# Another order of the fixed places in SBUF: parts and sums of activations three 64-byte lines under the weights

## The chip, the cores and the metric

The kernel runs on one NeuronCore of a Trainium2 chip. The metric is the time of one execution on the device in microseconds (us), lower is better; 0.2% of it is 1.3 us.

## The reference, cut to what matters

Causal attention over a window of 96 keys plus 8 global keys, with a slope per head, for 4 batches of 768 tokens and 8 heads of 64; its output, 3072 tokens of 512 features, goes through two matrix products with an ELU between them.

```python
scores = q @ k.T / 8 + bias          # 4 x 8 heads, 768 x 768, kept: 96 back or the first 8
a = softmax(where(keep, scores, -1e9))
x = (a @ v) laid out as 3072 x 512
h = x @ w_in                         # 512 -> 2048
g = where(h > 0, h, exp(min(h, 0)) - 1)
out = g @ w_out                      # 2048 -> 512
```

## The kernel before, in words

**Precision.** Every float32 operand of the two large products is split into a high part (`HI`, fp32r) and a rest (`LO` or "l"), and three of the four products of parts are added in PSUM. So x lives as `xh` and `xl`, each weight row block as one tile of 2 x 512 values, and the activations as pairs too.

**Tiling.** The 3072 tokens are 12 groups of 256. d_ff = 2048 is 16 blocks of 128 (`fc`). "Up" for one block (`mm1`) is 12 matmuls of 256 columns: the weights `w1` are the stationary operand (128x128), x is the moving one. "Down" makes the activations stationary and streams the second weights. Groups 0 to 3 use `moe` (up on L856, down on L885 with 512 moving columns, activations in `gh`, `gl`). Groups 4 to 11 use `seven` (up on L713, down on L769): two blocks make a pair, whose 2x2 products of quarters are formed with seven products, from activations in `rh`, `rl` (parts) and their sums in `sh`, `sl`, and from weights or mixes of weights (`mix`). A pair is 24 up matmuls and then 21 down matmuls of 256 columns; 8 groups have 64 pairs. Attention visits (values on L611, scores on L475) come in between, in the middle of an up or a down stretch.

**Order.** `Plan.order` is a list scheduler: it knows costs, due times and, for every class of tile, a list of named places (`SLOTS`). A tile takes the place that comes free first, ties by name. It never sees an address. The instructions are then issued in that order on every engine, under a manual schedule.

**Addresses.** Two pools lie behind each other in SBUF: `w` with the 32 weight tiles of 4096 bytes per partition, and `m`. `places_in_sbuf` allocates in `m` one tile per entry of `PLACES`, in the order of that list, so the list fixes the address of each name. Counted in bytes per partition, modulo 512: the weights and `pa0` to `pa5` (mixes of weights among them) start at the same remainder. `qk0` has 2496 bytes, which is 39 lines of 64 bytes, one line less than a multiple of 512. So each place from `xh0a` to `ph2` starts one line under the weights. The names that matter:

- `xh0*`, `xh1*`, `xl0*`, `xl1*`: x of groups 0, 1 and of groups 4 to 11 in turn
- `x0`, `ph2`, `rk0`, `va0`: x of group 3 (and sums before they are cast, scratch of attention)
- `xh2*`, `xl2*`: x of group 2; from group 4 on `sh` and `sl`
- `gh0` to `gh2`, `gl0` to `gl2`: `gh` and `gl`; from group 4 on `rh` and `rl`

Of the kernel before, what the change touches and what calls it, by code (L numbers as in the profile page):

```python
# [246 lines left out]
class Kernel:  # L247
# [686 lines left out]
    def build(self):  # L934
# [63 lines left out]
        for _, f in sorted(todo, key=lambda x: x[0]):  # L998
# [5 lines left out]
    LATE, FIRST_LOADS = 12, 22  # L1004
    RESUMED = 4
    PLACES = (("pa0", 2048), ("pa1", 2048), ("pa2", 2048), ("pa3", 2048), ("pa4", 2048), ("pa5", 2048), ("qk0", 2496), ("xh0a", 2048), ("xh0b", 2048),
# [5 lines left out]
    PREPARE, SE = (168000.0, 9000.0, 6000.0), 4  # L1012
    OF = ({1: (0, 0), 2: (0, 1), 6: (1, 0), 5: (1, 1), 3: (2, 0), 7: (2, 1), 4: (3, 0)}, {1: (0, 0), 4: (0, 1), 6: (1, 0), 7: (2, 0), 2: (3, 0), 5: (4, 0), 3: (5, 0)})
    ON_PE = []
# [355 lines left out]
```

## Time and profile before

| | us |
|---|---|
| runs, median (lowest to highest of 3) | 634.79 (634.67 to 634.83) |
| profiled execution, its own time | 634.52 |
| its span, first to last instruction | 632.7 |
| PE busy | 621.9 |

The span is what the trace holds; 1.8 us of the profiled execution lie around it. In the tables PE is TensorE's matmul row and PEld its loads of stationary operands, which run beside the matmuls. "The chain" is the chain of work that ended last, followed back from the last instruction; in it a stretch of matmuls is told by the starts, so its length divided by its count is the time from one matmul to the next.

### The profile page before, as it was taken

What the parts mean: (1) busy time and instruction counts of PE and PEld (TensorE: products, weight loads), DVE (VectorE), ACT (ScalarE), POOL (GpSimd) and SP (SyncE); (2) the same over time, 40 slices, a digit from 0 to 9 for tenths busy, and PEclk for the clock granted to TensorE, in tenths of its full rate; (3) what the DMA queues carried; (4) which work ended last, traced back from release to release, by engine and by line L of the source; (5) the groups of instructions that cost most, each with busy time, mean ns of one, the idle gap of its engine ahead of it and who ended that gap; (6) DMA issues with size and microseconds to landing.
All of it is one profiled execution on the core that took longest, in us unless ns stands there. A gap on an engine that the chain in (4) does not pass through costs nothing.

```text
span 632.7 us, 19150 instructions
## 1 busy us (share of the span) xinstructions
PE 621.9 (98%) x7046; PEld 576.7 (91%) x7046; DVE 487.8 (77%) x1630; ACT 428.3 (68%) x1246; POOL 207.7 (33%) x491
## 2 busy tenths in 40 slices
PE   8999999999999999999999999999999999999995
PEld 5778888898898889999999999999999999999995
DVE  6899888878786877777877877877877877875755
ACT  5999778888656755667667667667667666655552
POOL 3645465656464784112112112112112112110000
PEclk9999999999999999999999999999999999999999
DMA  8979835322354899998898898998997997994542
GB/s 306 383 274 408 318 129 137 114 68 88 89 199 155 268 301 271 304 273 266 280 271 252 266 272 276 280 272 259 274 276 249 279 282 250 261 247 153 183 151 87
DMA packets 131171, 149.82 MB, mean 237 GB/s; under 512 B 63616, under 2 KB 82816, under 8 KB 131072
## 3 DMA queue, kind: packets, MB, share of 16 engines
q1 hardware_dynamic: 130784, 148.41, 74.9%
q8 instruction: 57, 0.93, 0.6%
q14 instruction: 42, 0.34, 0.2%
q10 hardware_dynamic: 288, 0.13, 0.1%
HBM read 117.57 MB, written 30.93 MB: 235 GB/s over the span
## 4 chain that ended last, share of the span: by engine, by line
PE 92%; DVE 3%; ACT 2%; issue 1%; DMA 1%; POOL 0%; ACTq 0%; DVEq 0%; POOLq 0%
PE h L713 28%; PE o L769 25%; PE h L856 13%; PE o L885 13%; PE s L611 5%; PE s L475 4%; PE pv L508 2%; PE t L528 1%; PE t L530 1%; DMA n_raw<-in_n_dram 1%; PE none L1141 1%; ACT pt L304 0%; ACT pr L465 0%; DVE g L397 0%; DVE hl L673 0%
## 5 line engine op out<-in xcount | busy, mean ns | idle before, releaser
L581 POOL TENSOR_SCALAR pr<-pr,st 128x168 f32<-128x168 f32 x144 | 74.1, 515 | 254.0 <-DVE st L483 197.5
L713 PE MATMUL h<-xh,w 128*128 128x256 f32 x1024 | 138.8, 278 | 0.0
L713 PEld LDWEIGHTS h<-xh,w 128*128 128x128 f32 x1024 | 127.7, 188 | 0.3
L723 DVE SCALAR_TENSOR_TENSOR gg<-e,h 128x256 f32<-128x256 f32 x128 | 53.6, 418 | 83.6 <-ACT e L722 83.5
L465 ACT ACTIVATE pr<-pr,nmax 128x168 f32<-128x168 f32 x192 | 82.8, 432 | 25.0 <-DVE nmax L463 24.7
L856 PEld LDWEIGHTS h<-xh,w 128*128 128x128 f32 x512 | 76.0, 188 | 9.8 <-DVE gl L312 0.6
L721 ACT ACTIVATE e<-h 128x256 f32<-128x256 f32 x128 | 49.0, 383 | 52.3 <-PE h L713 52.3
L885 PE MATMUL o<-w,gh 128*128 128x512 f32 x256 | 80.4, 399 | 0.4 <-ACT o L304 0.4
L856 PE MATMUL h<-xh,w 128*128 128x256 f32 x512 | 80.2, 282 | 0.2 <-DVE gl L312 0.2
L713 PE MATMUL h<-xl,w 128*128 128x256 f32 x512 | 79.8, 278 | 0.0
L713 PEld LDWEIGHTS h<-xl,w 128*128 128x128 f32 x512 | 68.3, 188 | 0.5 <-issue 0.2
L312 POOL TENSOR_TENSOR w<-g,w 128x256 fp32r<-128x256 f32 x64 | 50.2, 807 | 41.2 <-ACT w L304 20.5
L304 ACT CAST sh<-sum 128x512 fp32r<-128x512 f32 x64 | 39.9, 623 | 34.2 <-DVE sum L737 34.2
L463 DVE CUSTOM_DVE_ANT_0 pr<-s,far 128x168 f32<-128x168 f32 x192 | 53.5, 321 | 2.3 <-PE s L475 0.8
L722 ACT ACTIVATE e<-e 128x256 f32<-128x256 f32 x128 | 53.3, 416 | 2.8
L304 ACT CAST rh<-gg 128x384 fp32r<-128x384 f32 x64 | 33.0, 515 | 27.7 <-DVE gg L723 27.6
L586 DVE STREAM_TRANSPOSE tr<-pr 128x192 f32<-128x192 f32 x144 | 51.2, 366 | 0.5 <-POOL pr L581 0.3
L769 PE MATMUL o<-mix,sh 128*128 128x256 f32 x256 | 51.1, 281 | 0.0
L769 PE MATMUL o<-w,sh 128*128 128x256 f32 x256 | 50.6, 287 | 0.0
L312 DVE TENSOR_TENSOR sl<-sum,sh 128x512 fp32r<-128x512 f32 x64 | 43.7, 682 | 7.1 <-ACT sh L304 7.1
L885 PEld LDWEIGHTS o<-w,gh 128*128 128x128 f32 x256 | 42.9, 189 | 6.6 <-ACT o L304 0.8
L885 PE MATMUL o<-w,gl 128*128 128x512 f32 x128 | 45.0, 396 | 0.0
(141 smaller groups left out, 1390.7 us busy)
## 6 DMA issues: line engine op xcount, KB each, us to landing
mix<-mixed SPq DMA_DIRECT2D x192, 256.0 KB, 3.8
qk<-in_qkv_dram SPq DMA_DIRECT2D x48, 312.0 KB, 4.0
v<-in_qkv_dram SPq DMA_DIRECT2D x36, 384.0 KB, 4.8
dd<-tr SPq DMA_DIRECT2D x36, 384.0 KB, 4.1
pt<-dd SPq DMA_DIRECT2D x72, 192.0 KB, 4.0
bits<-in_w_in_dram SPq DMA_DIRECT2D x16, 512.0 KB, 7.6
bits<-in_w_out_dram SPq DMA_DIRECT2D x16, 512.0 KB, 9.4
mixed<-mix SPq DMA_DIRECT2D x32, 256.0 KB, 3.7
```

The costliest lines, as they stand in the source:

```text
L304: self.nc.scalar.copy(out, x)
L312: self.on(e).tensor_tensor(out, x, y, ALU.subtract)
L463: first = p.add((("DVE", 85 + 1.042 * LW, False),), lambda e: nc.vector.tensor_tensor_reduce(x(), s.t[:, i, :LW], tab, -(2.0 ** -(h + 1)), ...
L465: p.add(act(LW, extra=200), lambda e: nc.scalar.activation(x(), x(), AF.Exp, bias=nm, scale=-1.0, accum_out=st.t[:, n, 0:1]), [pr], [pr, s ...
L581: nc.gpsimd.tensor_scalar(pr.t[:, :LW], pr.t[:, :LW], st.t[:, n, 3:4], 1.0, ALU.mult, ALU.mult)
L586: nc.vector.transpose(tr.t[:, :, i, j], pr.t.rearrange("p (b r) -> p b r", r=32))
L713: nc.tensor.matmul(h.t, w1.t[:, s, cc * P:(cc + 1) * P], self.chunk(x, cc), start=n == 0 and s == HI and cc == 0, stop=n == 1 and cc == se ...
L722: p.add(act(W), lambda e: nc.scalar.activation(ex.t, ex.t, AF.Exp, scale=-1.0), [ex], [ex], d - 8000)
L723: p.add(dve(W), lambda e: nc.vector.scalar_tensor_tensor(gs(), ex.t, -1.0, h.t, ALU.add, ALU.max), [h, ex], [g], d - 8000)
L769: nc.tensor.matmul(acc[bank].t[:, half], a, b.t[:, LO if t == 1 else HI, x], start=j == 0 and t == 0 and n in first, stop=j == self.NFC // ...
L856: nc.tensor.matmul(h.t, w1.t[:, s, cc * P:(cc + 1) * P], self.chunk(x, cc), start=n == 0 and cc == 0, stop=n == 2 and cc == self.NCC - 1)
L885: nc.tensor.matmul(o.t[:, :at.stop - at.start], g.t[:, i * P:(i + 1) * P], w2.t[:, s, at], start=fc == f0 and n == 0 and s == HI and not r ...
```

## The change

Only the order of `PLACES` changes. The tiles of x of groups 0 and 1 and the five places `rk0`, `va0`, `x0`, `ph2`, `rqv0` come first, and `xh2*`, `xl2*`, `gh*`, `gl*` follow behind `rqv0`. Sizes, names, `SLOTS`, due times and the program are as before.

```diff
-    PLACES = (... ("qk0", 2496), ("xh0a", 2048), ("xh0b", 2048),
-             ("xh1a", 2048), ("xh1b", 2048), ("xh2a", 2048), ("xh2b", 2048), ("xl0a", 2048), ("xl0b", 2048), ("xl1a", 2048), ("xl1b", 2048),
-             ("xl2a", 2048), ("xl2b", 2048), ("gh0", 1536), ("gh1", 1536), ("gh2", 1024), ("gl0", 1536), ("gl1", 1536), ("gl2", 1024), ("rk0", 2048),
-             ("va0", 2048), ("x0", 2048), ("ph2", 2496), ("rqv0", 2496), ("tf0", 1024), ...
+    PLACES = (... ("qk0", 2496), ("xh0a", 2048), ("xh0b", 2048),
+             ("xh1a", 2048), ("xh1b", 2048), ("xl0a", 2048), ("xl0b", 2048), ("xl1a", 2048), ("xl1b", 2048), ("rk0", 2048), ("va0", 2048),
+             ("x0", 2048), ("ph2", 2496), ("rqv0", 2496), ("xh2a", 2048), ("xh2b", 2048), ("xl2a", 2048), ("xl2b", 2048), ("gh0", 1536),
+             ("gh1", 1536), ("gh2", 1024), ("gl0", 1536), ("gl1", 1536), ("gl2", 1024), ("tf0", 1024), ...
```

In front of the moved tiles there are now three tiles of 2496 bytes (`qk0`, `ph2`, `rqv0`) in place of one: 117 lines, three less than a multiple of eight. So `xh2*`, `xl2*`, `gh*` and `gl*` start three lines under the weights. `xl0*`, `xl1*` move by 4096 bytes and `rk0`, `va0`, `x0`, `ph2`, `rqv0` by 16384, both multiples of 512, and keep their remainder. Everything from `tf0` on stays where it was.

## Rows read from the trace of the kernel before

**Rows 1.** The page: span, busy time of PE, its clock by slices, the chain by engine.
```profile
span 632.7 us, 19150 instructions
...
PE 621.9 (98%) x7046; PEld 576.7 (91%) x7046; DVE 487.8 (77%) x1630; ACT 428.3 (68%) x1246; POOL 207.7 (33%) x491
...
PEclk9999999999999999999999999999999999999999
...
PE 92%; DVE 3%; ACT 2%; issue 1%; DMA 1%; POOL 0%; ACTq 0%; DVEq 0%; POOLq 0%
```

**Rows 2.** Busy time of each engine in two stretches: us, instructions, clock, DMA share, GB/s.
```profile
257.00:520.00 263.00, 263.00 (x3334) 255.26 (x3331) 203.24 (x737) 172.89 (x510) 51.52 (x176) 1.00 0.91 271
...
576.00:625.00 49.00, 48.97 (x422) 48.55 (x421) 31.23 (x92) 25.87 (x60) 0.00 (x0) 1.00 0.47 152
```

**Rows 3.** Groups of PE by line and shape: count, busy us, mean ns, idle before.
```profile
L713 PE MATMUL h<-xh,w 128*128 128x256 f32 x1024 | 138.8, 278 | 0.0
L885 PE MATMUL o<-w,gh 128*128 128x512 f32 x256 | 80.4, 399 | 0.4 <-ACT o L304 0.4
L856 PE MATMUL h<-xh,w 128*128 128x256 f32 x512 | 80.2, 282 | 0.2 <-DVE gl L312 0.2
...
L885 PE MATMUL o<-w,gl 128*128 128x512 f32 x128 | 45.0, 396 | 0.0
L856 PE MATMUL h<-xl,w 128*128 128x256 f32 x256 | 40.4, 280 | 0.0
...
L611 PE MATMUL s<-pt,v 64*64 64x64 f32 x1728 | 33.4, 222 | 0.0
```

**Rows 4.** The chain from 259 to 300 us: start, us, line and count.
```profile
264.22 0.94 PE h L713 x8
...
266.60 2.04 PE h L713 x16
268.63 2.38 PE o L769 x21
271.02 2.83 PE h L713 x24
273.85 2.47 PE o L769 x21
276.32 2.73 PE h L713 x24
279.05 1.70 PE o L769 x15
...
282.19 0.91 PE o L769 x6
283.09 2.73 PE h L713 x24
```

**Rows 5.** The chain from 575 to 634 us, after the last attention visit.
```profile
581.58 2.83 PE h L713 x24
584.41 2.47 PE o L769 x21
586.88 2.73 PE h L713 x24
...
608.04 2.73 PE h L713 x24
610.78 2.38 PE o L769 x21
613.16 2.83 PE h L713 x24
```

**Rows 6.** Groups of PE in the up stretch from 289.87 to 292.60 us.
```profile
L713 PE MATMUL h<-xh,w 128*128 128x256 f32 x16 | 2.1, 277 | 0.0
L713 PE MATMUL h<-xl,w 128*128 128x256 f32 x8 | 1.2, 276 | 0.0
```

**Rows 7.** Groups of PE in the next up stretch, from 294.98 to 297.81 us.
```profile
L713 PE MATMUL h<-xh,w 128*128 128x256 f32 x16 | 2.2, 281 | 0.0
L713 PE MATMUL h<-xl,w 128*128 128x256 f32 x8 | 1.3, 281 | 0.0
```

6 rows, old and new, of the table PLACES are left out of this document.

## The prediction

> **What bounds the kernel.** I began with the page. PE is busy for 621.9 of 632.7 us, the chain that ended last is 92% PE, and the granted clock is 9 in every slice, so TensorE keeps its upper level of 2.4 GHz [rows 1]. The stretches say the same: between 257 and 520 us PE never pauses, and near the end neither [rows 2]. The groups by line show no wait worth a term in front of the large matmuls (at most 0.4 us in all) [rows 3]. So nothing that another engine does is worth time here; what counts is how fast one matmul follows another. For that I read the chain as a list of stretches, and there the reader should see something odd: the same 24 up matmuls take 2.73 us in one pair and 2.83 in another, the same 21 down matmuls 2.38 or 2.47 [rows 4, 5]. Per matmul that is 113 to 114 ns against 118. I call these the quick and the slow pace. In a slow stretch the matmul itself is longer, 281 ns against 276 or 277, with no idle time before it [rows 6, 7]: the operand stream is held up.
>
> Three things about the two paces matter. **They last**: a stretch keeps its pace, and an up stretch hands it to the next down stretch (2.83 then 2.47) [rows 4, 5]. **They swap at the step from down to up**: a quick down (2.38) is followed by a slow up (2.83), a slow down (2.47) by a quick up (2.73), and after the last attention visit the pairs simply alternate [rows 5]. **A down that resumes after an attention visit is slow**, 0.91 us for 6 (152 ns each, the restart included), and a quick up follows; an up resumed after a visit ends 16 in 2.04 us and its down is quick [rows 4]. In the chain from 257 us to the end I count 59 up stretches of 24: 17 slow (the first at 271.02, the last at 613.16); 33 whole down stretches: 16 slow; and 28 visits that cut a stretch, one of them an up (of the 1728/48 = 36 visits [rows 3], the rest are earlier).
>
> **The change part by part.** *The program* is not touched: the planner sees names, no addresses, so all instructions, waits and DMA issues stay in their order on every queue. Nothing is added or removed, and no DMA reads or writes a moved tile. Cost 0 by construction. *ACT, DVE and POOL*, which write and read the moved tiles, see addresses that differ by a multiple of 64 bytes. I take 0; the cover is that PE waits for them 0.0 to 0.4 us per group [rows 3], and if a cast got slower by a few ns it would still be hidden. *TensorE's operands* are the only term. In lines of 64 bytes, modulo eight and counted from the weights: an up matmul has stationary 0 and moving -1, before and after (only group 2 gets moving -3). A down matmul has moving 0 and stationary -1 before, -3 after. So relative to the moving operand the stationary one goes from +1 (up) and -1 (down) to +1 and -3. The trace has only the first two, and both have a quick and a slow pace. No row shows what -3 does, so I bound it.
>
> Late part, from 257 us (64 pairs). A slow up costs 2.83 - 2.73 = 0.10 us, a slow down 2.47 - 2.38 = 0.09 [rows 4]. Below: all quick gives back 17 x 0.10 + 16 x 0.09 = 3.1 us. A visit inside a down costs 1.70 + 0.91 - 2.38 = 0.23, one inside an up 0.94 + 2.04 - 2.73 = 0.25 [rows 4], although the up is quick again soon; so hardly more than 0.03 of each is pace, 28 x 0.03 = 0.8. Together -3.9 us. Above: all slow adds (64 - 17) x 0.10 = 4.7 for the ups, 17 x 0.09 = 1.5 for the whole quick downs and, for the 28 cut ones, 15 x 0.0043 = 0.06 each, 1.8. Together +8.0 us.
>
> Early part (groups 0 to 3). The up matmuls of L856 average 282 and 280 ns [rows 3], at the slow 281 [rows 7], so there is little left to lose and 768 x 4.2 ns (0.10 us / 24) = 3.2 us to gain. The 384 down matmuls of L885 have no quick row to compare with; at the same 4.2 ns each they may give or take 1.6. Bounds -4.8 and +1.6 us. I take -0.6: runs of 4 to 8 matmuls switch often, as now, so I stay near zero.
>
> A pace quicker than 113 ns is in no row of 64 x 45 = 2880 late matmuls; I can't exclude it and leave it to the low end of the range.
>
> **What I take for the late part.** The step from down to up loads the same first weights (0) against the same moving operand (0), before and after. So I expect a quick down still to throw the next up into the slow pace. What is open is the step from up to down, where the first load reads line -3 over a stream of line -1, and whether -3 holds a slow pace. Three outcomes are near each other: pairs alternate as now (0); all ups quick and all downs slow, 64 x 0.09 = 5.8 against the present 3.9, +1.9; all ups slow and downs quick, 64 x 0.10 = 6.4, +2.5. Their mean is +1.5, with the early -0.6 it is +0.9 us. The sum is made against the profiled execution, 634.52 (span 632.7 and 1.8 around it); the median of the runs is 0.27 above it. 634.8 + 0.9 = **635.7 us**. This forecast's own range is 633.2 (alternating, early part -1.6) to 637.7 (late +2.5, early +0.4).
>
> **The rivals.**
>
> *All quick, faster.* If -3 leaves no place for the slow pace in a down, or the step from down to up no longer meets it at the wrong moment, most slow stretches go. For it: the pace of a stretch is decided by where its neighbour left it, and the change alters exactly one of the two relations. Against: the relation at the step where quick turns slow is not altered. Late -3.9, early -1.5: 629.4 us; from about -1.3 us on it is this case.
>
> *Resumed downs turn quick, and the ups pay: slower.* The place is the piece of 6 to 12 down matmuls behind an attention visit. Today it is slow, and that is why the next up is quick. If with -3 the piece regains the quick pace, as a resumed up does now, it saves 0.03 us, but the next up is slow (+0.10) and hands that to its down up to the next visit (15 x 0.0043 = +0.06): +0.14 net, 28 times, +3.9; with +0.5 early 639.2 us. It decides once the piece is quick at its last matmul. If the slow pace then stays through down to up as well, the bound is all slow, +8.0 + 1.6 = 644.4.
>
> *Nothing happens.* The two paces may hang on the moment at which a stretch begins and not on addresses at all; then the change does nothing that it says, 634.8 us. For it: the same addresses run at both paces [rows 6, 7]. Against: up and down, which differ only in operands and addresses, swap the pace in a fixed way [rows 5]. The Trainium skill (TensorE: Matmul & The Clock Gate, Step-by-step: what each phase is for) says that loads and the moving operand have independent read ports and that "Loading the next tile's weights doesn't steal SBUF read bandwidth from the running matmul"; by it the sum would be 634.8 too, and addresses could not matter. That matmuls with no wait in front of them stretch from 276 to 281 ns [rows 6, 7] does not fit that rule well.
>
> **How the numbers follow.** My forecast gets 0.38, all quick 0.31, the ups that pay 0.23, nothing 0.08. A measurement of this kernel tells about 0.2%, 1.3 us, from no change. The forecast's own range is divided at those bounds: 0.05 faster, 0.21 within, 0.12 slower. So faster 0.05 + 0.31 = 0.36; within 0.2% 0.21 + 0.08 = 0.29; slower 0.12 + 0.23 = 0.35. The likeliest case lies inside 0.2%, with cases of both signs beside it. The range 629.0 to 641.0 leaves out about a third of the fast case (between 629.4 and the bound of -8.7, or a pace that no row shows) and some four tenths of the slow one (toward 644.4), 0.10 and 0.09.
>
> **What would show it.** Counts by line and the order must be as before, and the waits in front of PE too. In the chain, count the up stretches at 2.73 and 2.83 and the down stretches at 2.38 and 2.47: forecast about half of them slow; all quick shows 2.73 and 2.38 throughout; the slow rival shows the pieces behind a visit at some 0.88 us for 6 and more than 40 ups at 2.83. L856's mean at 282 says that the early part did not move. The prediction is wrong if a stretch shows a length outside these four, if stretches change pace in their middle, or if the time goes by more than 1.3 us while the paces stay; then an engine other than TensorE felt the addresses.

## The result, and the profile after

| | before | after |
|---|---|---|
| runs, median (lowest to highest of 3), us | 634.79 (634.67 to 634.83) | 639.05 (638.99 to 639.30) |
| profiled execution, its own time / span, us | 634.52 / 632.7 | 639.05 / 637.3 |
| whole ups in the chain from 257 us, quick / slow | 42 / 17 | 32 / 27 |
| whole downs, quick / slow | 17 / 16 | 1 / 32 |

These counts, like those of the prediction and of the tables below, are made in windows of the chain of 45 to 90 us, and a stretch that lies over a window's edge is not in them: of the 61 whole ups and 34 whole downs from 257 us on, 59 and 33 are. Read in one piece, the chain has no step that goes another way than the counted ones.

The change made the kernel slower: the ratio of the comparison is 1.0051 (95% interval 1.0026 to 1.0076); the quotient of the medians, 1.0067, lies inside it. The time is inside the predicted range, but 3.35 us above the predicted value, and on the other side of the 0.2% bound.

The page of the changed kernel, the lines that answer to [rows 1]:

```profile
span 637.3 us, 19150 instructions
...
PE 626.4 (98%) x7046; PEld 580.3 (91%) x7046; DVE 488.7 (77%) x1630; ACT 427.5 (67%) x1246; POOL 206.9 (32%) x491
...
PEclk9999999999999999999999999999999999999998
...
PE 92%; DVE 3%; ACT 2%; issue 1%; DMA 1%; POOL 0%; DVEq 0%; ACTq 0%; POOLq 0%
```

Instructions, counts and order on each engine are those of before; the clock is at its upper level throughout. PE is busy 4.5 us longer and the span is 4.6 us longer. The other engines' busy times moved by at most 0.9 us. The same 263 us as in [rows 2], with the same columns:

```profile
257.00:520.00 263.00, 263.00 (x3327) 254.93 (x3318) 202.97 (x736) 171.15 (x507) 51.71 (x176) 1.00 0.89 268
```

PE has no pause in it, as before, and gets 7 matmuls fewer done (3327 against 3334): no wait was added, the matmuls follow each other less quickly. The groups of PE by line and shape, to be read against [rows 3]:

```profile
L713 PE MATMUL h<-xh,w 128*128 128x256 f32 x1024 | 139.7, 279 | 0.0
L885 PE MATMUL o<-w,gh 128*128 128x512 f32 x256 | 80.9, 400 | 0.4 <-ACT o L304 0.4
L856 PE MATMUL h<-xh,w 128*128 128x256 f32 x512 | 80.2, 282 | 0.1
...
L885 PE MATMUL o<-w,gl 128*128 128x512 f32 x128 | 45.1, 396 | 0.0
L856 PE MATMUL h<-xl,w 128*128 128x256 f32 x256 | 40.7, 281 | 0.0
L769 PE MATMUL o<-w,rh 128*128 128x256 f32 x256 | 40.6, 280 | 0.0
```

The idle column stays near zero. The mean of L713 rose from 278 to 279 ns; L856's of 282 stands still. Means over a mixture of two paces hide most of it, so the chain is the view to read. The chain of the changed kernel, from 269 to 299 us and near its end, for [rows 4, 5]:

```profile
269.39 2.39 PE o L769 x21
271.78 2.83 PE h L713 x24
274.61 2.48 PE o L769 x21
277.09 2.74 PE h L713 x24
279.83 1.76 PE o L769 x15
...
289.95 0.88 PE o L769 x6
290.84 2.83 PE h L713 x24
293.67 2.48 PE o L769 x21
296.14 2.74 PE h L713 x24
...
604.63 2.47 PE o L769 x21
607.10 2.74 PE h L713 x24
609.84 2.47 PE o L769 x21
612.32 2.74 PE h L713 x24
```

Three things differ. A quick up (2.74) is now followed by a slow down (2.47, or 1.76 for 15), where the down used to keep the quick pace (1.70 for 15 in [rows 4]). Behind the last visit the pairs no longer alternate; every up is quick and every down slow. And behind a visit's piece of 6 the next up is slow, where it was quick.

**Where it went.** Counted from the first matmul of the trace, the first one on L713 starts 0.59 us later (244.58 against 244.00 us) and the last one on L769 4.26 us later (628.90 against 624.64). So some 0.6 us came in the early part and 3.7 in the late one. The start stamps agree for the late part and give more for the early one: the sum of what each large matmul takes above 113.33 ns (226.67 for 512 columns; longer ones than 12 ns above left out) rose in the late part from 5.2 to 9.0 us (ups 2.6 to 4.0, downs 2.6 to 5.0) and in the early part from 3.9 to 5.1.

The piece behind a visit shows most in single matmuls. From the start stamps, the time from one matmul to the next in the commonest piece of 6 (the first value holds the restart), and the length of the up behind it:

```
before  228 120 117 118 117 117   then 2.73
after   223 116 118 122 119 113   then 2.83
```

Of 27 such pieces (20 of 6 and 7 of 12) 26 ended slow before; now 25 end at 113 or 114 ns. Each of these 25 has a slow up behind it, and so had the one quick piece of before. In 12 of the 20 pieces of 6 the pace turns inside the piece, as in the row above, where the last matmul alone is quick.

### The profile page after: what moved, and what is told of

Read it like the earlier page. It is cut to its first block, busy times and chain, and to the rows that moved or that the text cites. A ratio compares the mean times of both kernels' runs of the same rounds, so it can differ in the third digit from the quotient of the medians.

```text
span 637.3 us, 19150 instructions
## 1 busy us (share of the span) xinstructions
PE 626.4 (98%) x7046; PEld 580.3 (91%) x7046; DVE 488.7 (77%) x1630; ACT 427.5 (67%) x1246; POOL 206.9 (32%) x491
## 4 chain that ended last, share of the span: by engine, by line
PE 92%; DVE 3%; ACT 2%; issue 1%; DMA 1%; POOL 0%; DVEq 0%; ACTq 0%; POOLq 0%
PE h L713 28%; PE o L769 25%; PE o L885 13%; PE h L856 13%; PE s L611 5%; PE s L475 4%; PE pv L508 2%; PE t L528 1%; PE t L530 1%; DMA n_raw<-in_n_dram 1%; PE none L1141 0%; ACT pt L304 0%; ACT pr L465 0%; DVE g L397 0%; DVE ob L799 0%
## 5 line engine op out<-in xcount | busy, mean ns | idle before, releaser
L713 PE MATMUL h<-xh,w 128*128 128x256 f32 x1024 | 139.7, 279 | 0.0
L713 PEld LDWEIGHTS h<-xh,w 128*128 128x128 f32 x1024 | 128.5, 189 | 0.4
L856 PEld LDWEIGHTS h<-xh,w 128*128 128x128 f32 x512 | 75.8, 188 | 10.2 <-DVE gl L312 0.5
L885 PE MATMUL o<-w,gh 128*128 128x512 f32 x256 | 80.9, 400 | 0.4 <-ACT o L304 0.4
L856 PE MATMUL h<-xh,w 128*128 128x256 f32 x512 | 80.2, 282 | 0.1
L713 PE MATMUL h<-xl,w 128*128 128x256 f32 x512 | 80.2, 279 | 0.0
L713 PEld LDWEIGHTS h<-xl,w 128*128 128x128 f32 x512 | 68.5, 188 | 0.5 <-issue 0.2
L769 PE MATMUL o<-mix,sh 128*128 128x256 f32 x256 | 51.6, 283 | 0.0
L769 PE MATMUL o<-w,sh 128*128 128x256 f32 x256 | 50.9, 288 | 0.0
L885 PEld LDWEIGHTS o<-w,gh 128*128 128x128 f32 x256 | 42.9, 188 | 6.8 <-ACT o L304 0.8
L885 PE MATMUL o<-w,gl 128*128 128x512 f32 x128 | 45.1, 396 | 0.0
```

The lines of the kernel that those rows point to most:

```text
L713: nc.tensor.matmul(h.t, w1.t[:, s, cc * P:(cc + 1) * P], self.chunk(x, cc), start=n == 0 and s == HI and cc == 0, stop=n == 1 and cc == se ...
L769: nc.tensor.matmul(acc[bank].t[:, half], a, b.t[:, LO if t == 1 else HI, x], start=j == 0 and t == 0 and n in first, stop=j == self.NFC // ...
L856: nc.tensor.matmul(h.t, w1.t[:, s, cc * P:(cc + 1) * P], self.chunk(x, cc), start=n == 0 and cc == 0, stop=n == 2 and cc == self.NCC - 1)
L885: nc.tensor.matmul(o.t[:, :at.stop - at.start], g.t[:, i * P:(i + 1) * P], w2.t[:, s, at], start=fc == f0 and n == 0 and s == HI and not r ...
```

## The experiments

All of them move places only; the program and the planner's order stay. I write a place's **line** as its start in lines of 64 bytes from the second weights and mixes, modulo four (why four is enough is a result below): before has first weights 0, x -1, parts and sums -1. The **load** of a stretch is the line of the stationary operand minus that of the streamed one: +1 in an up and -1 in a down before, +1 and +1 in the changed kernel, because -3 and +1 are the same modulo four. Four sets, each on one chip with its own runs of the kernel before. The places of attention (`qk0`, `rqv0`) move too in some of them, but an attention visit keeps its length: from the last large matmul in front to the first one behind, the mean is 1.637 to 1.640 us in all fourteen kernels.

| kernel | load up / down | whole ups (us) | whole downs (us) | median us | ratio (95%) |
|---|---|---|---|---|---|
| before | +1 / -1 | 42 at 2.73, 17 at 2.83 | 17 at 2.38, 16 at 2.47 | 634.79 | |
| after | +1 / +1 | 32 at 2.74, 27 at 2.83 | 1 at 2.39, 32 at 2.47 | 639.05 | 1.0051 (1.0026 to 1.0076) |
| sums3 | +1 / -1 parts, +1 sums | 24 at 2.74, 34 at 2.83 | 14 at 2.38, 19 at 2.42 | 637.71 | 1.0035 (1.0021 to 1.0049) |
| parts3 | +1 / +1 parts, -1 sums | 51 at 2.73, 7 at 2.83 | 1 at 2.39, 32 at 2.47 | 637.59 | 1.0033 (1.0018 to 1.0047) |
| all3 | -1 / +1, x moved | 35 at 2.72, 23 at 2.83 | 15 at 2.40, 18 at 2.48 | 637.72 | 1.0044 (1.0027 to 1.0061) |
| x0 | 0 / -1 | 59 at 2.88 | 32 at 2.38 | 641.87 | 1.0108 (1.0088 to 1.0128) |
| x4_parts_m1 | 0 / -1 | 59 at 2.88 | 32 at 2.38 | 641.00 | 1.0096 (1.0079 to 1.0113) |
| x4_parts3 | 0 / -1 | 59 at 2.88 | 33 at 2.38 | 641.30 | 1.0100 (1.0083 to 1.0117) |
| parts0 | +1 / 0 | 58 at 2.74 | 33 at 2.50 | 638.81 | 1.0063 (1.0046 to 1.0080) |
| split_w1 | +1 / +1, one stream line | 23 at 2.72, 36 at 2.83 | 8 at 2.38, 25 at 2.47 | 638.06 | 1.0049 (1.0035 to 1.0063) |
| split_w2 | 2 / 2, one stream line | 58 at 2.85 | 31 at 2.49 | 646.16 | 1.0182 (1.0169 to 1.0195) |
| split_w3 | -1 / -1, one stream line | 1 at 2.72, 58 at 2.83 | 32 at 2.47 | 642.61 | 1.0119 (1.0104 to 1.0134) |
| split_13 | +1 / -1, one stream line | 59 at 2.72 | 33 at 2.38, 1 at 2.47 | 631.90 | 0.9955 (0.9941 to 0.9968) |
| split_31 | -1 / +1, one stream line | 36 at 2.72, 23 at 2.83 | 33 at 2.38 | 634.43 | 0.9994 (0.9985 to 1.0003) |

"One stream line" means that x and the second weights share a line; lengths within 0.02 us stand together. The kernel before had medians of 635.21, 635.11, 635.06 and 634.71 in the four sets.

### The change in halves: sums alone, parts alone

sums3 (`xh2*`, `xl2*` moved, `gh*`, `gl*` left):

```diff
-             ... ("xl1b", 2048), ("xl2a", 2048), ("xl2b", 2048), ("gh0", 1536), ... ("x0", 2048), ("ph2", 2496), ("rqv0", 2496), ("tf0", 1024), ...
+             ... ("x0", 2048), ("gh0", 1536), ... ("gl2", 1024), ("ph2", 2496), ("rqv0", 2496), ("xh2a", 2048), ... ("xl2b", 2048), ("tf0", 1024), ...
```

> Only the sums (and x of group 2) lie three lines under the weights, the parts stay one line under. Theory A, the step: the pace that a down stretch takes over from the up before it is set by the line of its first load, a part, against the line of x that streams meanwhile (equal before, two lines apart in the change). Here the first load is as before, so a quick up (2.73 us) is followed by a quick down (2.38), pairs alternate after the last visit, and the time is that of before, 634.8 within 1.5 us. Theory B, the relation inside the down: at three lines a down matmul tends to the slow pace by itself. Then the 12 of 21 matmuls on sums are slow in most downs, about half of the loss: some 637.

parts3 (`gh*`, `gl*` moved, `xh2*`, `xl2*` left):

```diff
-             ... ("xl2b", 2048), ("gh0", 1536), ... ("gl2", 1024), ("rk0", 2048), ("va0", 2048), ("x0", 2048), ("ph2", 2496), ("rqv0", 2496), ("tf0", 1024), ...
+             ... ("xl2b", 2048), ("rk0", 2048), ("va0", 2048), ("x0", 2048), ("ph2", 2496), ("rqv0", 2496), ("gh0", 1536), ... ("gl2", 1024), ("tf0", 1024), ...
```

> Only the parts lie three lines under the weights, sums stay one line under. Theory A: the first load of a down is a part, so nearly all downs turn slow as in the change, also their matmuls on sums: downs at 2.47 us, 638 to 639.5. Theory B: 9 of 21 matmuls slow, stretches of about 2.42 us and some 636.5.

**Measured.** 637.71 and 637.59 us: each half alone is slower than before, by 0.35% and 0.33%. In parts3 every quick up is followed by a slow down: 25 of 25 whole downs, and all 23 first pieces. Near its end the chain reads:

```profile
600.20 2.73 PE h L713 x24
602.93 2.47 PE o L769 x21
```

So the slow downs of the change come from the parts, whose first tile is what a down loads first. In sums3 a down behind a quick up stays quick (13 of 13), but a down behind a slow up turns quick in its middle. The chain of sums3 shows the new length, 2.42:

```profile
272.25 2.83 PE h L713 x24
275.08 2.42 PE o L769 x21
277.50 2.83 PE h L713 x24
```

And the groups of PE in that one down, from 275.08 to 277.49 us, show where it turns:

```profile
L769 PE MATMUL o<-mix,sh 128*128 128x256 f32 x4 | 0.8, 276 | 0.0
L769 PE MATMUL o<-w,sh 128*128 128x256 f32 x4 | 0.7, 276 | 0.0
L769 PE MATMUL o<-w,rh 128*128 128x256 f32 x4 | 0.6, 280 | 0.0
L769 PE MATMUL o<-mix,sl 128*128 128x256 f32 x2 | 0.6, 277 | 0.0
...
L769 PE MATMUL o<-w,rl 128*128 128x256 f32 x2 | 0.4, 280 | 0.0
```

The parts (`rh`, `rl`), loaded from line -1, run at the slow 280 ns; the sums (`sh`, `sl`), loaded from +1, at the quick 276. The streams (`w`, `mix`) are the same for both. So **a load that goes from -1 to +1 under an unmoved stream makes a slow pace quick**; 19 of 19 such downs did so. The down then ends quick, and the next up is slow (30 of 30), as in the kernel before. That is why sums3 costs time although its downs are the better ones. The reset by itself brings nothing. Theory A had the step behind a quick up right in both halves, but it missed the turn in the middle and with it the time of sums3 (634.8 expected). Theory B named that time (some 637) for the opposite reason: it had the matmuls on sums at the slow pace, and they run at the quick one.

### x moved as well, and x on the weights' line

```diff
# all3: x, parts and sums three lines under
-             ... ("pa5", 2048), ("qk0", 2496), ("xh0a", 2048), ...
+             ... ("pa5", 2048), ("qk0", 2496), ("ph2", 2496), ("rqv0", 2496), ("xh0a", 2048), ...
# x0: x on the weights' line, parts and sums one line under
+             ... ("pa5", 2048), ("xh0a", 2048), ... ("xl1b", 2048), ("rk0", 2048), ("va0", 2048), ("x0", 2048), ("ph2", 2496), ("xh2a", 2048), ... ("gl2", 1024), ("qk0", 2496), ("rqv0", 2496), ...
```

> Inputs, parts and sums all lie three lines under the weights, so a down has the relation of the change to its own moving operand, but its first load again has the line of x. Theory A: a quick or slow up hands its pace to the down again, ups and downs of a pair are alike, and the time is near before, 634.8 within 2 us. Theory B: downs slow as in the change, 638 or more.

> Inputs lie at the line of the weights (except group 2), parts and sums one line under them. Theory A with its second half, that a step changes the pace because the streams of up (x) and down (weights and mixes) lie on different lines: here both stream from the same line, nothing shifts at a step, and after a quick start nearly all stretches stay quick, 2.73 and 2.38: 629 to 631.5. Theory B says nothing of inputs; the down relation is that of before, so 634.8 within 1.5 us. Against both: an up whose load and stream lie on the same line may hold no quick pace, ups at 2.83 or more, 638 or more.

**Measured.** all3 took 637.72 us, which neither theory's account gives: restoring the distance between x and the parts doesn't restore the time. Its steps are the mirror image of before. From down to up the pace is kept (13 of 13 quick or nearly quick, 17 of 17 slow), from up to down it swaps (17 of 17 quick ups have a slow down, 14 of 15 slow ups a down that is quick but for its first matmuls). In whole stretches, whatever decides is at a step between two streams.

x0 took 641.87 us, where I had expected a gain: a clear miss. Its chain near the end:

```profile
603.45 2.88 PE h L713 x24
606.33 2.38 PE o L769 x21
608.71 2.88 PE h L713 x24
```

Every whole down is quick, as hoped, but every up runs at 2.88/24 = 120.0 ns, a third pace that no row of before has. Groups of PE in one of these ups, from 603.46 to 606.32 us:

```profile
L713 PE MATMUL h<-xh,w 128*128 128x256 f32 x16 | 2.2, 283 | 0.0
L713 PE MATMUL h<-xl,w 128*128 128x256 f32 x8 | 1.3, 283 | 0.0
```

283 ns for a matmul, against 276 and 281 [rows 6, 7], again with no idle time. In x0 an up streams x from the same line from which it loads its weights.

### Modulo eight or four, and the third pace in a down

`pr0` and `pr1` have 768 bytes, 12 lines, so one in front of x puts x four lines above the weights.

```diff
# x4_parts_m1: x four lines above, parts and sums one line under
+             ... ("pa5", 2048), ("pr0", 768), ("xh0a", 2048), ... ("ph2", 2496), ("pr1", 768), ("xh2a", 2048), ... ("gl2", 1024), ("qk0", 2496), ("rqv0", 2496), ...
# x4_parts3: the same without pr1 in front of xh2a, so parts and sums three lines above
+             ... ("ph2", 2496), ("xh2a", 2048), ... ("gl2", 1024), ("qk0", 2496), ("rqv0", 2496), ("pr1", 768), ...
# parts0: parts and sums on the weights' line, x one line under as before
+             ... ("pa5", 2048), ("gh0", 1536), ... ("gl2", 1024), ("xh2a", 2048), ... ("xl2b", 2048), ("qk0", 2496), ("xh0a", 2048), ... ("xl1b", 2048), ("rk0", 2048), ...
```

> Inputs of groups 0, 1, 3 and 4 to 11 lie four lines above (which is four lines under, modulo eight) the line of the weights, parts and sums one line under as before. With inputs at the line of the weights all downs were quick (2.38 us), even behind slow ups, but the ups had a third pace of 2.88 us. Theory C: the quick pace of a stretch starts at a fixed moment of a 6.67 ns beat which is set by the line of the moving operand, 1.67 ns (four matmul columns) per line, so it repeats after four lines; streams that agree modulo four lines do not lose the pace at a step. The third pace comes from load and stream on the same line. If that needs the same line modulo eight, ups here are quick too: 2.73 and 2.38 throughout, 629 to 631.5. If modulo four is enough, ups take 2.88 again: 640 to 642. Against theory C (inputs four lines off behave like inputs one line off): pairs alternate, 634.8 within 2.

> Inputs four lines above the line of the weights, parts and sums three above, so one under the inputs. Theory C with the third pace modulo eight: steps lose nothing, ups 2.73, downs 2.38, 629 to 631.5; the pieces behind visits may differ from 0.91. With the third pace modulo four: ups 2.88, 640 to 642. If the relation of the down's own operands (+3 in place of -1) matters for the pace it takes at a step, downs at 2.47, some 634.

> Parts and sums lie at the line of the weights (x of group 2 too), the other inputs one line under. Theory C: a down now loads and streams from the same line, so it has the third pace, 21 in some 2.52 us; 64 x 0.14 us more than quick downs. Ups follow an unaligned down and are quick or slow: 637 to 642. If the third pace of the ups came from something else (the repeated weights), downs are at 2.38 or 2.47 and the time is 632 to 637.

**Measured.** 641.00 and 641.30 us, with ups of 2.88 and downs of 2.38: four lines away is as bad as none, and three lines above does what one line under does. So in both of these pairs the lines count modulo four, 256 bytes. parts0 took 638.81 us, all ups quick and all whole downs at 2.50/21 = 119.0 ns: the third pace belongs to a load of 0, in a down as in an up.

### First weights apart from the second ones

To put x and the second weights on one line and yet load neither weights nor activations from it, the two sets of weights have to stand on different lines. `places_in_sbuf` gets, in front of its loop:

```diff
     def places_in_sbuf(self):
+        for which, pad in ((1, 64), (0, 192)):
+            for fc in range(self.NFC):
+                self.w.tile([P, 2 * self.DM], F32, tag=f"w{which}{fc}", name=self.n("place"))
+            self.w.tile([P, pad // 4], F32, tag=f"pad{which}", name=self.n("place"))
```

The second weights (`w1*`) come first, then the first ones (`w0*`) one line higher, then a filler. split_w2 and split_w3 have `(1, 128), (0, 128)` and `(1, 192), (0, 64)`. x is placed as in x0, and parts and sums stand behind `qk0`, `rqv0` (split_w1), behind `qk0` (split_w2) or ahead of both (split_w3), on +1, 2 and -1.

> The first weights (stationary in up) lie one line above the second weights and mixes (moving in down); inputs at the line of the second weights, parts and sums one line above it (three under, modulo four; x of group 2 too). Theory C with lines modulo four: all streams share one line, so no step loses the pace, and no load shares the line of its stream, so there is no third pace. Ups 2.73, downs 2.38 except behind visits: 629 to 631.5, faster than before by 0.5 to 0.9%. If a slow stretch behind a visit carries its pace through the steps as well, since nothing resets it now, a large part stays slow: 634 to 641. Rival: the pace at a step hangs on which tile is loaded first and not on the agreement of the streams; then as the change, 637 or more.

> As with one line, but first weights, parts and sums two lines off the streams. Theory C: steps lose nothing, no third pace; at two lines, the farthest that four allow, the slow pace may not exist at all, then everything is quick also behind visits: 626 to 630. If two lines off still holds the slow pace and nothing resets it: 634 to 641.

> As before, but first weights, parts and sums three lines above (one under) the streams. Theory C: steps lose nothing and there is no third pace. Downs behind a visit were slow to the end with parts one line under; nothing resets them here, so slow pieces go on into ups and downs until the next visit: between 630 and 638, worse than one line above.

**Measured.** 638.06, 646.16 and 642.61 us: no gain. With equal loads of +1 or -1 and one stream line nothing changes the pace at a step. In split_w1 all 7 quick whole downs have a quick up behind them and all 23 slow downs a slow up; from up to whole down 8 of 8 and 24 of 24 keep it. The rival, that the tile loaded first decides and not the agreement of the streams, expected a quick up to have a slow down behind it, and falls with the 8. In split_w3 almost every stretch is slow, to the end:

```profile
604.76 2.83 PE h L713 x24
607.59 2.47 PE o L769 x21
610.06 2.83 PE h L713 x24
612.89 2.47 PE o L769 x21
```

So in whole stretches the slow pace is not a disturbance that dies away. It lasts until a step resets it or a visit interrupts it. split_w2 adds a fourth pace: a load of 2 gives 2.85/24 = 118.8 ns in the whole ups and 2.49/21 = 118.6 in the downs, so two lines apart is no escape either. Its 646.16 us are outside what I had expected, and so are the 642.61 of split_w3 (630 to 638).

### A reset at each pair

```diff
# split_13: first weights +1 (pads 64, 192 as above), x 0, parts and sums -1
+             ... ("pa5", 2048), ("xh0a", 2048), ... ("x0", 2048), ("ph2", 2496), ("xh2a", 2048), ... ("gl2", 1024), ("qk0", 2496), ("rqv0", 2496), ...
# split_31: first weights -1 (pads 192, 64), x 0, parts and sums +1
+             ... ("ph2", 2496), ("qk0", 2496), ("rqv0", 2496), ("xh2a", 2048), ... ("gl2", 1024), ...
```

> First weights one line above, x and second weights (with the mixes) on the common line, parts and sums one line below. All streams then share a line, so no step shifts the phase; what changes at a step is only whether the load is one line above or one below the stream. Theory (pace is a phase that a first load can reset): at the step from down to up the load goes from one below to one above its stream, the change that turned slow downs quick in their middle when only the sums were moved. So every up is quick whatever ran before it (all of about 59 whole ups at 2.74), downs keep what the up gave them (2.38), and only the pieces behind a visit may be slow: 630 to 632 us. Rival (a stretch keeps its pace whenever the streams share a line, as with the first weights one line above and everything else on that side): slow pieces hand their pace on, most whole ups and downs of a visit's neighbours slow: 636 to 640. Second rival (the other direction, from one above to one below, turns quick to slow, as the changed kernel's step from up to down did): all ups 2.74 and all downs 2.47, 636 to 638.

> The mirror image: first weights one line below, x and second weights on the common line, parts and sums one line above. Theory: the reset now lies at the step from up to down (load from one below to one above the stream), so every down that begins behind an up is quick (about 33 whole ones at 2.38), a slow piece behind a visit hands its pace to one up (2.83) and no further: some 25 ups slow of 59, others quick, 632 to 635 us. Rival (pace kept at each step): as with three lines of the other sign, nearly all ups at 2.83 and downs at 2.47, 640 to 643. Second rival (from one above to one below turns quick to slow): all ups at 2.83 and all whole downs at 2.38, 636 to 639.

**Measured.** split_13 took 631.90 us, **faster than both kernels** (0.9955 of before, 0.9941 to 0.9968), and split_31 634.43, no change (0.9985 to 1.0003). Both are in the band that the theory gave, at its upper end, and neither rival's. The chain of split_13 around a visit and near its end:

```profile
282.14 0.91 PE o L769 x6
283.05 2.72 PE h L713 x24
285.77 1.70 PE o L769 x15
...
602.84 2.38 PE o L769 x21
605.22 2.72 PE h L713 x24
607.93 2.38 PE o L769 x21
```

and its row for the 263 us of [rows 2]:

```profile
257.00:520.00 263.00, 263.00 (x3405) 254.78 (x3397) 204.09 (x742) 173.38 (x512) 51.24 (x176) 1.00 0.91 271
```

A piece behind a visit is still slow (0.91 for 6), but the up behind it is quick, and the pace holds to the next visit. PE gets 71 matmuls more done in those 263 us than before. Of the 5.2 us of late excess 1.6 are left.

Part of that is a new wait. At each of the seven changes of group the first matmul of a down takes 177 to 180 ns to the next one, and the rest of its piece is slow (1.83 us for 15 in place of 1.70). The view of waits names nothing there, but the order of time does:

```profile
302.32 0.74 DVE L799 TENSOR_TENSOR ob<-ob,o 128x256 f32<-128x256 f32 x2
302.57 0.69 PE L769 MATMUL o<-w,rh 128*128 128x256 f32 x4
```

The four additions on L799 read the accumulators of the group that has just ended, while PE begins the next group. By the single stamps the third of them ends 164 to 169 ns after the start of that first matmul, and the second matmul starts 9 to 15 ns after this end. all3 and split_31 have the same hold seven times, split_w1 once: in all 22 cases the second matmul starts 7 to 18 ns after the third addition has ended. In the other 76 changes of group, over all kernels, the third addition ends at most 71 ns after the first matmul's start, and nothing is held (113 to 122 ns). So a quicker TensorE runs into VectorE here; whether a semaphore or the accumulator itself holds it, the profile doesn't tell. It costs 6 x 0.13 + 0.10 = 0.9 us, of which the hold itself, about half, is not in the sum of excess, and some 0.4 us of slow matmuls is.

In split_31 the reset lies at the other step: each of the 23 pieces that end slow hands its pace to one up (I had expected some 25), and then the down is quick (13 of 13 whole ones behind a slow up):

```profile
282.66 0.90 PE o L769 x6
283.56 2.83 PE h L713 x24
286.39 1.70 PE o L769 x15
```

## What decides the pace

**The load sets which paces there are.** 0 gives only 119 to 120 ns, 2 only 118.6 to 118.8, and +1 or -1 either 113.3 to 114.2 or some 117.8 (a stretch's length by its count). Here are the steps with their counts of whole stretches in the chain (pieces where named):

| kernel, step | stream's line | load | quick becomes | slow becomes |
|---|---|---|---|---|
| before, up to down | -1 to 0 | +1 to -1 | quick 16/16 | slow 16/16 |
| before, down to up | 0 to -1 | -1 to +1 | slow 16/16, piece 1/1 | quick 15/15, pieces 26/26 |
| after, up to down | -1 to 0 | +1 to +1 | slow 17/17 | slow 15/15 |
| after, down to up | 0 to -1 | +1 to +1 | slow 1/1, pieces 25/25 | quick 29/29, pieces 2/2 |
| split_w1, both | stays | +1 to +1 | quick 15/15 | slow 47/47 |
| split_w3, both | stays | -1 to -1 | | slow 60/60 |
| split_13, up to down | stays | +1 to -1 | quick 33/33 | |
| split_13, down to up | stays | -1 to +1 | quick 30/30 | quick, pieces too |
| split_31, up to down | stays | -1 to +1 | quick 19/19 | quick 13/13 |
| split_31, down to up | stays | +1 to -1 | quick 31/31, pieces 4/4 | slow, pieces 23/23 |
| sums3, inside a down | stays | -1 to +1 | quick 13/13 | quick 19/19 |

(Pieces are those behind a visit, sorted by their last matmul.) With the stream on one line, a load that stays or goes from +1 to -1 keeps the pace, and one from -1 to +1 ends quick. When the stream's line moves too, the result is another, and in the change it is the bad one: at the step from up to down both paces end slow.

**What a piece behind a visit takes is only half explained.** The pieces of 6 load nothing but sums. With a load of -1 nearly all of them end slow: 20 of 20 in before and in parts3, 19 in split_w3, at least 16 in split_13. With a load of +1 the number that ends quick goes from 2 of 20 in sums3 and 3 in split_31 to 14 in all3 and split_w1 and 18 in the changed kernel. And the pace can turn inside such a piece, with no step and every load on one line, as it does in 13 of the 20 in split_w1. So what a restart gives hangs on more than the load, and what else stays open. It matters for the change: sums alone or parts alone leave 18 and 20 of the 20 slow, only both together make them quick, and 25 of the change's 27 slow ups stand behind quick pieces.

**Why a stream's line matters at a step** is seen in the start stamps. A quick matmul takes 113.33 ns (113, 113 and 114 in turn), which is 17 times 6.667 ns (16 columns at 2.4 GHz), and 120.0 is 18 times that. Starts of matmuls inside a stretch with a quick one in front of them and quick themselves, between 257 and 420 us counted from the first matmul, by their remainder to 6.667 ns in seven bins of 1 ns (the last one narrower):

```
before    up   257   0   0   0   0   0 141
before    down   0 180  90   0   0   0   0
split_13  up     0   0   0   0 341 252   0
split_13  down   0   0   0   0 214 154   0
```

In each row they fall on one place of the beat, as near as stamps of whole ns tell. With x one line under the second weights, ups and downs have places some 1.7 ns apart; with both on one line they share it; in all3, with x one line above, they are 1.7 ns apart the other way. So a step between streams of different lines moves the phase at which the quick matmuls start, by a quarter of a beat for one line. That much the stamps show. That a first load which meets the stream badly is what costs or restores the pace is my reading of it and not shown, and what inside the chip has this beat stays open.

The Trainium skill (TensorE: Matmul & The Clock Gate, Step-by-step: what each phase is for) says that loading the next weights takes no SBUF read bandwidth from the running matmul. Taken as the whole story, that leaves a placement no way to move the time; twelve of them, with the same instructions, lie between 631.90 and 646.16 us, and the matmul's own duration goes from 276 to 283 ns with the line of the load. Here the measurement decides.

## Why the prediction came out as it did

**What bounds the kernel: right.** Nothing but the pace of TensorE moved. Idle time in front of the large matmuls stayed at 0.0 to 0.4 us a group, the program's order stayed, and the four lengths of a whole stretch are the four that I read before. Of my signs of being wrong one did come, though only in pieces behind a visit: there the pace turns in the middle. That "the operand stream is held up" was more than the rows said; they show a longer matmul with no idle time in front.

**The step from down to up: right.** I had it unchanged, a quick piece or down followed by a slow up. 26 of 26 did so, and the slow downs have a quick up behind them (29 of 29 whole ones).

**The step from up to down: the one that failed.** I left open whether -3 keeps a quick pace there, took three outcomes with a mean of +1.5 us, and priced "all ups quick and all downs slow" at +1.9. It does not keep it: 17 of 17 quick ups have a slow whole down. That outcome came true for the downs, and behind the last visit for the ups as well. But the forecast kept the pieces behind a visit as they were, and there the slow rival's mechanism came in: 25 of 27 pieces end quick, and the up behind them pays. It was put there as a case apart from slow downs; the two came together, and why the pieces end quick is open, as said above. So the ups are not all quick, 27 of 59 are slow.

The late term in its own prices: 10 more slow ups x 0.09 = 0.9; 16 more slow downs x 0.09 = 1.4; the 19 pieces of 15 ahead of a visit, 1.76 against 1.70, 1.1; the 7 of 9 ahead of one, 1.06 against 1.02, 0.3. That is +3.7. The pieces behind a visit give back some 0.5 (the 7 of 12 mostly 1.56 against 1.61, those of 6 up to 0.03). The stamps have +3.8 in all, so some 0.6 is outside these whole stretches and pieces, in rounding and cut ups. I had +1.5. (The prediction's bounds also took all 64 pairs for the stretch from 257 us on; 61 whole ups and one cut one lie there.)

**The early term: the wrong sign.** I took -0.6; the first matmul of L713 starts 0.6 us later. The two early sums of excess rose by 0.5 (L856) and 0.65 (L885), 1.15 together, so not all of it reached the end of that part. It is inside my bounds. "L856's mean of 282 says that the early part did not move" was too coarse a sign: 0.5 us over 768 matmuls is 0.7 ns each.

**The rivals.** The slow rival was nearest in the sum, 639.2 against 639.05, by a mechanism that did occur, but its account was incomplete: it had the quick piece's slow up hand its pace on, and "more than 40 ups at 2.83". The slow down behind that up is slow anyway, and the next up is quick. So there were 10 more slow ups and not 28, and 16 more slow downs that it had not priced made up for the rest: that its sum agrees to 0.15 us is luck. All quick fell: it needed -3 to leave no slow pace, and a load of +1 has both. That the change does nothing fell too. Behind the +1.5 stood one shortcut: I treated -3 as something no row shows. Modulo four it is +1, the load of an up, and the trace had both paces of that; that four is the modulus only the later runs showed. And the +1.5 was the mean of three outcomes with equal weight, none of which came as it stood.

**Not tried:** a placement for the early part (groups 0 to 3). It holds 3.9 to 5.8 us of excess in every kernel here, also in the fastest (4.4).

## What to carry to other kernels

Where TensorE never waits, read the chain as lengths of equal stretches: two lengths for the same count are a term of their own, and here it was worth 14 us, 2%, between the best and the worst placement of the same program. As far as this one kernel shows (fp32r operands, 256 columns, 128 rows): keep what is loaded and what is streamed one line of 64 bytes apart modulo 256, never on the same line or two apart, and put all streams on one line, so that a step from one product to the next leaves the phase alone. That alone is no gain (638.06 and 642.61 us): choose the signs so that a slow stretch is reset often, weights of the product that follows a visit's remainder one line above the stream, activations of the other one line below, as in split_13. And when TensorE has become quicker, look again for waits that it did not have before.

## What the runs showed that was not expected

- A pace is a state: with no reset at a step the slow one went on through all 60 counted steps between whole stretches of split_w3, some 118 against 113 ns, with nothing waiting.
- Lines count modulo four: x at 0 and at +4 gave 641.87 and 641.00 to 641.30 us, with the same ups of 2.88.
- A load on the line of the running stream costs 120.0 ns a matmul, 18 beats of 6.667 ns for the quick pace's 17; two lines apart costs 118.8.
- The early matmuls of 512 columns hardly react: L885's excess over 226.67 ns stayed between 1.3 and 2.2 us for 384 matmuls in all kernels.
